# A new order for the last unit of a convolution kernel: products 1, 3, 2, 4, 5, 7, 6, 0, the turn of the unit before it between its two parts, and three steps on other engines

## The chip, the cores and the metric

The kernel runs on one core of a Trainium2 chip. Five engines work side by side, each in its own written order: TensorE (PE, matmuls and transposes; its weight loads are shown as PEld), VectorE (DVE), ScalarE (ACT), GpSimd (POOL) and SyncE (SP), which here only issues DMAs. They wait for one another through semaphores. The metric is the device time of one execution in microseconds (us).

## The reference

x has the shape (2, 2048, 1024), w has (3, 1024, 1024); all is in bfloat16. The kernel computes a convolution over the sequence with three taps, then a batch norm with given mean and variance, then silu:

```python
xp = jnp.pad(x, ((0, 0), (P, P), (0, 0)))
y = sum(jnp.einsum('bsc,cd->bsd', xp[:, k:k + S, :], w[k]) for k in range(K))
inv_std = 1.0 / jnp.sqrt(var + 1e-5)
y = (y - mean) * (g * inv_std) + b
return _silu(y)
```

## The kernel before

The convolution is done in a fast form that makes 6 outputs from 8 inputs with 8 products in place of 18. The sequence is cut into 342 tiles of 6 positions (`M_OUT`); the last tile has only 2 positions inside the sequence. At the start the inputs of each batch are transformed: for each of the 8 points j a matmul against a small matrix gives `T_sb[bi][:, ct, j, tile]`, 8 channel chunks `ct` of 128. The weights are combined per chunk of 128 output channels into six combined sets (`wts`, tile `uch`); points 0 and 7 use the raw taps (`wch`).

A *unit* is one chunk of output channels (`dc`, 8 of them) for one batch (`bi`, 2): 16 units. A unit does eight products; product j is 8 matmuls (L250), one for each `ct`, which add up in one PSUM bank. PSUM is one tile, `ps_all`, of 8 banks of 512 columns. A unit uses four banks, A, B, C and G, and units alternate between banks 0 to 3 and 4 to 7. Products 1 and 2 go to A, 3 and 4 to B, 5 and 6 to C, 7 to G and 0 to A. Each of the three pairs gives a sum and a difference: the second product is added onto the first in the bank, and the first alone (`m1`, `m3`, `m5`) is copied out before that by ScalarE. From `m1` and A come `s1`, the sum, and `d1`, twice `m1` less the sum; for the other two pairs VectorE writes twice m less the bank back into the bank. VectorE then adds the pieces, with factors, into six outputs y[0] to y[5] (`scalar_tensor_tensor`, written `stt`). ScalarE applies the norm and silu in one ACTIVATE (`silu`, L261), into `yT` in bfloat16, with channels on the partitions. The outputs lie in `y` in the order 2, 4, 1, 3, 5, 0 (`ENDS`) in the last two units, so that `silu(..., 0, 2)` does outputs 2 and 4 and `silu(..., 2, 6)` the other four.

The result must be turned so that positions are on partitions. Units 1 to 14 are turned by a DMA transpose. The fifteenth unit and the last, sixteenth, are turned by TensorE (`turn_tiles`, L465): transposes of 128 by 128 into bfloat16 views of PSUM banks (`turn_view`; 768 bfloat16 elements are 384 columns of a bank), which are then copied to SBUF and stored by DMAs on SP's queue.

The kernel is written with a manual schedule: on every engine the instructions stand in the order in which the program issues them. Waits between engines follow from the tiles that are read and written, in program order.

The change lies in the last unit (L453 to L570). It is cut into two parts along the tiles: columns 0 to 228 (`cut` is 229) and columns 229 to 341 (113 of them). Both parts are written by the generator `last_part` (L478), which yields after every matmul; `run(gen, n)` takes n matmuls of it, with what stands between them. `hooks` names places where ScalarE gets a silu that was left over: the fifteenth unit's two silus (`late`), or those of the parts themselves. The last unit's first part uses banks 4 to 7 (`here`), its second part banks 0 to 3 (`there`), the banks in which the fifteenth unit was summed.

In the order of the program, before:

- First part, products 1, 3, 5, 2, 4, 6 and half of 7 (`run(first, 52)`). The fifteenth unit's silus stand ahead of `m1`'s copy and behind `s1`'s copy (L507). `d1` is made by VectorE (L506). VectorE's work on y follows from L510.
- The stores of unit 13 (five DMAs on SP's queue).
- The turn of the fifteenth unit: 18 transposes into the upper columns (128 to 511) of banks 0, 1 and 3 and three copies into `o_before` (named `o_sb` in the profile; L544), the first two by ScalarE, the third by VectorE.
- The rest of the first part: half of product 7, product 0.
- The fifteenth unit's stores (five DMAs on SP's queue, L410 and L414).
- Second part: the same eight products on 113 columns in banks 0 to 3, with the first part's silus ahead of `m3` and behind `s1`, and its own first silu after the even outputs.
- The turn of the last unit: three blocks of tiles, 0 to 127, 128 to 228 (both from the first part) and 229 to 341. Block 0 is copied by ScalarE, block 1 by VectorE (L562), and each is stored right behind its copy; the last block is copied by VectorE in three pieces (L566, L568, L569), outputs 2 and 4 first, and then stored.

`store_block` (L467) issues a block's rows on SP's queue in a multiple of 16; five rows that are left of block 1 and the two positions of the last tile go out from ScalarE's queue (L473, L476).

Of the kernel before, what the change touches and what calls it, by code (L numbers as in the profile page):

```python
# [9 lines left out]
ALU = mybir.AluOpType  # L10
# [17 lines left out]
ALPHA = -1.0 / 20.0  # L28
# [9 lines left out]
def kernel(  # L38
# [10 lines left out]
    nc = tc.nc  # L49
# [6 lines left out]
    NTB = (S + M_OUT - 1) // M_OUT  # L56
# [3 lines left out]
    NB = (NTB + P - 1) // P  # L60
# [182 lines left out]
    def mms(bk, j, dc, bi, c0, c1, start):  # L243

        for ct in range(CT):
            if j in (0, 7):
                lhsT = raw[dc][0 if j == 0 else 2][:, ct, :]
            else:
                lhsT = wts[dc][:, j - 1, ct, :]
            nc.tensor.matmul(  # L250
                ps_all[:, bk * 512:bk * 512 + c1 - c0],
                lhsT=lhsT,
                rhs=T_sb[bi][:, ct, j, c0:c1],
                start=start and ct == 0,
                stop=ct == CT - 1,
                skip_group_check=not start,
            )
            yield

    def silu(dc, yT, y_all, c0, c1, i0, i1, step=1):  # L260
        nc.scalar.activation(  # L261
            yT[:, i0:i1:step, c0:c1],
            y_all[:, i0:i1:step],
            ACT.Silu,
            bias=beta[:, dc:dc + 1],
            scale=sk[:, dc:dc + 1],
        )
# [71 lines left out]
    def run(gen, n=None):  # L339
        while n is None or n > 0:  # L340
            if next(gen, run) is run:
                return
            if n is not None:
                n -= 1

    units = [(dc, bi) for dc in range(DC) for bi in range(B)]
    late = []
    with tc.tile_pool(name="xwin", bufs=10) as xpool:
# [19 lines left out]
        first = unit(0, 0, 0, NTB, (0, 1, 2, 3), yTs[0], late, seven_first=True)  # L368
# [21 lines left out]
    def rows(bi, n0, n1):  # L390
        r0 = bi * S
        return out_f[r0 + n0 * M_OUT:r0 + n1 * M_OUT]
# [9 lines left out]
    def store_unit(dc, bi, block):  # L402

        dcols = slice(dc * P, (dc + 1) * P)
        for nb in range(NB):
            n0, n1 = nb * P, min((nb + 1) * P, FULL)
            cuts = [n0, n1] if (n1 - n0) % 16 == 0 else [n0, n1 - (n1 - n0) % 16, n1]
            for a, z in zip(cuts, cuts[1:]):
                dst = rows(bi, a, z)[:, dcols].rearrange("(n i) d -> n i d", i=M_OUT)
                nc.sync.dma_start(out=dst, in_=block(nb)[a - n0:z - n0])  # L410
        if S % M_OUT:
            n0 = (NB - 1) * P
            dst = out_f[bi * S + FULL * M_OUT:(bi + 1) * S, dcols].rearrange("(n i) d -> n i d", i=S % M_OUT)
            nc.sync.dma_start(out=dst, in_=block(NB - 1)[FULL - n0:FULL - n0 + 1, 0:S % M_OUT])  # L414
# [10 lines left out]
    for ui, (dc, bi) in enumerate(units[1:-1], 1):  # L425
        yT = yTs[ui % 2]
# [25 lines left out]
    dc, bi = units[-1]  # L452
    yT = yTs[(len(units) - 1) % 2]  # L453
    half = 4 * ((len(units) - 1) % 2)
    here, there = [half + k for k in range(4)], [4 - half + k for k in range(4)]
    dcols = slice(dc * P, (dc + 1) * P)

    def turn_view(bk, at=0):
        pv = ps_all[:, bk * 512 + at:bk * 512 + at + M_OUT * P // 2]
        return pv.bitcast(BF16).rearrange("p (i d) -> p i d", d=P)  # L460

    def turn_tiles(pv, yT, n0, n1, k0=0, k1=M_OUT):

        for k in range(k0, k1):
            nc.tensor.transpose(pv[0:n1 - n0, ENDS[k]], yT[:, k, n0:n1], ident)  # L465

    def store_block(n0, n1, o_end):  # L467
        n2 = min(n1, FULL)
        n3 = n2 - (n2 - n0) % 16
        for a, z, queue in ((n0, n3, nc.sync), (n3, n2, nc.scalar)):  # L470
            if z > a:
                dst = rows(bi, a, z)[:, dcols].rearrange("(n i) d -> n i d", i=M_OUT)
                queue.dma_start(out=dst, in_=o_end[a - n0:z - n0])  # L473
        if n1 > FULL:
            dst = out_f[bi * S + FULL * M_OUT:(bi + 1) * S, dcols].rearrange("(n i) d -> n i d", i=S % M_OUT)
            nc.scalar.dma_start(out=dst, in_=o_end[FULL - n0:FULL - n0 + 1, 0:S % M_OUT])  # L476

    def last_part(c0, c1, banks, y_all, hooks):  # L478

        nn = c1 - c0  # L480
        A, B_, C_, G = [ps_all[:, k * 512:k * 512 + nn] for k in banks]
        bA, bB, bC, bG = banks
        m1, m3, m5, s1, d1 = (epool.tile([P, NTB], FP32, name=n)[:, 0:nn] for n in ("m1", "m3", "m5", "s1", "d1"))
        y = [y_all[:, ENDS.index(i)] for i in range(M_OUT)]

        def stt(o, i0, f, i1, op1=ALU.add):
            nc.vector.scalar_tensor_tensor(out=o, in0=i0, scalar=f, in1=i1, op0=ALU.mult, op1=op1)  # L487

        def at(name):
            for f in hooks.get(name, ()):  # L490
                f()

        def mm(bk, j, start):
            return mms(bk, j, dc, bi, c0, c1, start)

        at("m1")
        yield from mm(bA, 1, True)
        nc.scalar.copy(m1, A)
        at("m3")
        yield from mm(bB, 3, True)  # L500
        nc.scalar.copy(m3, B_)  # L501
        at("m5")
        yield from mm(bC, 5, True)
        nc.scalar.copy(m5, C_)
        yield from mm(bA, 2, False)
        stt(d1, m1, 2.0, A, op1=ALU.subtract)  # L506
        nc.scalar.copy(s1, A)  # L507
        at("s1")
        yield from mm(bB, 4, False)
        for i, f in ((2, 4.0), (4, 16.0), (0, 1.0)):  # L510
            stt(y[i], B_, ALPHA * f, s1)
        stt(B_, m3, 2.0, B_, op1=ALU.subtract)
        yield from mm(bC, 6, False)
        for i, f in ((2, 0.25), (4, 0.0625), (0, 1.0)):
            stt(y[i], C_, BETA * f, y[i])
        at("y24")
        stt(C_, m5, 2.0, C_, op1=ALU.subtract)
        for i in (5, 1, 3):
            stt(y[i], B_, ALPHA * 2.0 ** i, d1)
        for i in (5, 1, 3):  # L520
            stt(y[i], C_, BETA * 0.5 ** i, y[i])
        yield from mm(bG, 7, True)
        nc.vector.tensor_tensor(y[5], G, y[5], op=ALU.add)
        yield from mm(bA, 0, True)
        nc.vector.tensor_tensor(y[0], A, y[0], op=ALU.add)
        at("y")


    cut = FULL - 7 * 16
    y1 = endpool.tile([P, M_OUT, cut], FP32, name="y_end0")  # L530
    blocks = [(n, min(n + P, cut)) for n in range(0, cut, P)]
    ends = [endpool.tile([P, M_OUT, P], BF16, name=f"o_end{k}") for k in range(len(blocks) + 1)]
    o_before = opool.tile([P, M_OUT, NB, P], BF16, name="o_sb")

    first = last_part(0, cut, here, y1, {"m1": late[0:1], "s1": late[1:2]})
    run(first, 52)
    while turned:
        store_unit(*turned.pop(0))
    for nb, bk in enumerate((there[0], there[1], there[3])):
        n0, n1 = nb * P, min((nb + 1) * P, NTB)  # L540
        pv = turn_view(bk, 512 - M_OUT * P // 2)
        turn_tiles(pv, yTs[len(units) % 2], n0, n1)
        copy = nc.vector.tensor_copy if nb == NB - 1 else nc.scalar.copy
        copy(o_before[0:n1 - n0, :, nb], pv[0:n1 - n0])  # L544
    run(first)
    store_unit(*units[-2], lambda nb: o_before[:, :, nb])

    y2 = epool.tile([P, M_OUT, NTB], FP32, name="y")[:, :, 0:NTB - cut]
    second = last_part(cut, NTB, there, y2, {
        "m3": [lambda: silu(dc, yT, y1, 0, cut, 0, 2)],  # L550
        "s1": [lambda: silu(dc, yT, y1, 0, cut, 2, 6)],
        "y24": [lambda: silu(dc, yT, y2, cut, NTB, 0, 2)],
    })
    run(second)
    for k, (n0, n1) in enumerate(blocks):
        turn_tiles(turn_view(here[k]), yT, n0, n1)
    nn = NTB - cut
    pv, rest = turn_view(here[2]), turn_view(here[3])
    turn_tiles(pv, yT, cut, NTB, 0, 2)
    for k, copy in enumerate((nc.scalar.copy, nc.vector.tensor_copy)):  # L560
        n0, n1 = blocks[k]
        copy(ends[k][0:n1 - n0], turn_view(here[k])[0:n1 - n0])  # L562
        store_block(n0, n1, ends[k])
        if k == 0:
            silu(dc, yT, y2, cut, NTB, 2, 6)
    nc.vector.tensor_copy(ends[2][0:nn, 2:5:2], pv[0:nn, 2:5:2])  # L566
    turn_tiles(rest, yT, cut, NTB, 2, 6)
    nc.vector.tensor_copy(ends[2][0:nn, 1:6:2], rest[0:nn, 1:6:2])  # L568
    nc.vector.tensor_copy(ends[2][0:nn, 0], rest[0:nn, 0])  # L569
    store_block(cut, NTB, ends[2])  # L570


# [28 lines left out]
```

## Time and profile before

| | us |
|---|---|
| median of 3 runs | 192.84 (192.5 to 193.61) |
| the profiled execution | 193.53 |
| its span, first to last instruction | 191.7 |
| TensorE busy | 180.0 |
| VectorE busy | 161.3 |
| first matmul of the last unit's first part, second part | 172.78, 180.55 |
| the last addition into y ends | 186.06 |
| last block's store issued | 187.89 |
| last bytes moved | about 190.2 |

Times on the page are microseconds from the span's start. In a line of the timeline stand the start, the length, the engine, the line of the kernel, the operation, what it writes and reads (partitions x elements) and how often it was merged; in brackets the idle time ahead of it on its engine, and what ended that. The chain is followed back from the last instruction to whatever released it. A line of the waits has who waited, for whom, the total, how many times and the longest. DMA-issuing instructions (SPq, ACTq) show the time of the issue, not of the transfer; when bytes move is seen in the DMA share of short stretches.

### The profile page before, as it was taken

To read this page: it belongs to the slowest core of one execution; us is meant where nothing else is said; L and a number is where in the kernel's file an instruction comes from. 1 tells how busy PE (TensorE), PEld (TensorE's weight loads), DVE (VectorE), ACT (ScalarE), POOL (GpSimd) and SP (SyncE) were. 2 spreads that over 40 slices of the span, in tenths; PEclk is the share of its full clock that TensorE was granted. 3 is DMA by queue.
4 is the path that set the end of the run, shared out by engine and by line. 5 is a ranking of instruction groups with operands and counts; after the bars stand their busy time and mean duration, and the time that the engine had idled before them with its cause. 6 is when DMAs were issued, how large, how long until landed. Compare 5 with 4: busy or idle time off the path is not lost.

```text
span 191.7 us, 3904 instructions
## 1 busy us (share of the span) xinstructions
PE 180.0 (94%) x1404; PEld 128.0 (67%) x1404; DVE 161.3 (84%) x347; ACT 122.6 (64%) x201; POOL 148.0 (77%) x89
## 2 busy tenths in 40 slices
PE   7579999999999999999999999999999999999960
PEld 3369688866666666666666666666666666669950
DVE  6557999987999699969996999699969987788981
ACT  3747878888287726873786287638755873635770
POOL 6359999999949996999699969996999699900000
PEclk9966999999999999999999999999999999999996
DMA  4999997990608387999292989783746465566425
GB/s 124 323 369 305 329 292 202 285 221 0 123 0 170 69 184 196 275 142 202 46 192 57 205 228 243 147 180 68 168 81 151 95 143 108 124 120 160 118 66 105
DMA packets 86759, 31.72 MB, mean 165 GB/s; under 512 B 73364, under 2 KB 82580, under 8 KB 86740
## 3 DMA queue, kind: packets, MB, share of 16 engines
q1 hardware_dynamic: 86637, 31.46, 70.1%
q8 instruction: 11, 0.18, 0.4%
q14 instruction: 8, 0.07, 0.1%
q10 hardware_dynamic: 103, 0.02, 0.0%
HBM read 14.82 MB, written 8.39 MB: 121 GB/s over the span
## 4 chain that ended last, share of the span: by engine, by line
PE 84%; DVE 6%; DMA 5%; ACT 2%; SPq 1%; issue 1%; DVEq 0%; ACTq 0%
PE ps_all L250 75%; PE ps_all L225 8%; DMA xw<-in_x_dram 5%; DVE T_sb L241 3%; ACT yT L261 1%; DVE y L487 1%; PE ps_all L465 1%; SPq L215 1%; DVE y L291 0%; SPq L90 0%; DVE d L487 0%; DVE ps_all L487 0%; DVE o_end L568 0%; ACT s L507 0%; ACT m L501 0%
## 5 line engine op out<-in xcount | busy, mean ns | idle before, releaser
L250 PE MATMUL ps_all<-T_sb,uch 128*128 128x342 bf16 (+2 forms) x816 | 123.0, 299 | 0.0
L250 PEld LDWEIGHTS <-uch 128*128 128x128 bf16 x816 | 77.0, 97 | 33.2 <-issue 0.2
L261 ACT ACTIVATE yT<-y,beta,sk 128x684 bf16<-128x684 f32 (+5 forms) x46 | 44.2, 960 | 30.3 <-DVE y L291 29.6
L250 PE MATMUL ps_all<-T_sb,wch 128*128 128x342 bf16 (+2 forms) x272 | 44.0, 300 | 0.2 <-DVE T_sb L241 0.2
L291 DVE SCALAR_TENSOR_TENSOR y<-ps_all,y 128x342 f32<-128x342 f32 x90 | 41.9, 507 | 1.7 <-PE ps_all L250 0.7
L173 POOL TENSOR_TENSOR uch<-e,wch 128x1024 bf16<-128x1024 f32 x16 | 33.8, 2134 | 10.8 <-PE ps_all L250 5.9
L173 POOL TENSOR_TENSOR uch<-e,w1x 128x1024 bf16<-128x1024 f32 x16 | 33.8, 2135 | 0.6
L225 PE MATMUL ps_all<-Rm,xw 128*128 128x168 bf16 (+1 forms) x272 | 31.2, 251 | 3.2 <-DMA xw<-in_x_dram 2.8
L173 POOL TENSOR_TENSOR uch<-eh,w1x 128x1024 bf16<-128x1024 f32 x16 | 33.8, 2132 | 0.6
L250 PEld LDWEIGHTS <-wch 128*128 128x128 bf16 x272 | 25.6, 97 | 11.5 <-DVE T_sb L241 0.4
L239 ACT CAST T_sb<-ps_all 128x672 bf16<-128x672 f32 (+5 forms) x45 | 26.3, 606 | 9.4 <-PE ps_all L225 8.3
L298 ACT COPY m<-ps_all 128x342 f32<-128x342 f32 x45 | 19.9, 442 | 19.0 <-PE ps_all L250 18.3
L241 DVE CAST T_sb<-ps_all 128x672 bf16<-128x672 f32 (+3 forms) x40 | 26.3, 698 | 5.6 <-PE ps_all L225 5.2
L225 PEld LDWEIGHTS <-xw 128*128 128x128 bf16 (+1 forms) x272 | 24.6, 106 | 8.5 <-DMA xw<-in_x_dram 3.5
L291 DVE SCALAR_TENSOR_TENSOR y<-ps_all,d 128x342 f32<-128x342 f32 x45 | 20.3, 507 | 0.5
L163 POOL TENSOR_TENSOR e<-wch,w2x 128x1024 f32<-128x1024 bf16 x8 | 17.0, 2130 | 0.2
L163 POOL TENSOR_TENSOR eh<-w0x,wch 128x1024 f32<-128x1024 bf16 x8 | 17.1, 2132 | 0.1
L291 DVE SCALAR_TENSOR_TENSOR y<-ps_all,s 128x342 f32<-128x342 f32 x30 | 14.0, 508 | 3.2 <-ACT s L298 3.2
L291 DVE SCALAR_TENSOR_TENSOR d<-m,ps_all 128x342 f32<-128x342 f32 x15 | 7.6, 507 | 9.3 <-ACT s L298 9.3
L291 DVE SCALAR_TENSOR_TENSOR ps_all<-m,ps_all 128x342 f32<-128x342 f32 x30 | 15.3, 509 | 0.0
L169 DVE TENSOR_REDUCE e<-wch 128x1024 f32<-128x2048 bf16 x6 | 13.7, 2277 | 0.0
L298 ACT COPY s<-ps_all 128x342 f32<-128x342 f32 x30 | 13.1, 438 | 0.0
(65 smaller groups left out, 83.4 us busy)
## 6 DMA issues: line engine op xcount, KB each, us to landing
xw<-in_x_dram SPq DMA_DIRECT2D x30, 256.0 KB
out_dram<-o_sb SPq DMA_DIRECT2D x30, 192.0 KB
wch<-in_w_dram SPq DMA_DIRECT2D x9, 512.0 KB
out_dram<-o_sb SPq DMA_DIRECT2D x15, 120.0 KB
wch<-in_w_dram SPq DMA_DIRECT2D x6, 256.0 KB
xw<-in_x_dram SPq DMA_DIRECT2D x2, 224.0 KB
out_dram<-o_sb SPq DMA_DIRECT2D x15, 7.5 KB
out_dram<-o_sb SPq DMA_DIRECT2D x15, 0.5 KB
```

Of the source, the lines that this page charges most:

```text
L163: engine.tensor_tensor(e, a, c, op=ALU.add)
L169: nc.vector.tensor_reduce(e, taps.rearrange("p k ct d -> p ct d k"), axis=mybir.AxisListType.X, op=ALU.add)
L173: nc.gpsimd.tensor_tensor(wts[dc][:, 2 * n + (op == ALU.subtract)], outer[dc, n], odd, op=op)
L215: nc.sync.dma_start(out=xw[0:kk, :], in_=x[bi, t_lo:t_hi + 1, :])
L225: nc.tensor.matmul(banks[:, at:at + NJ * ntile], lhsT=xw[0:kk, (ct0 + c) * P:(ct0 + c + 1) * P], rhs=Rm[0:kk, :, 0:ntile], start=True, sto ...
L239: nc.scalar.copy(dst, src)
L241: nc.vector.tensor_copy(dst, src)
L250: nc.tensor.matmul(ps_all[:, bk * 512:bk * 512 + c1 - c0], lhsT=lhsT, rhs=T_sb[bi][:, ct, j, c0:c1], start=start and ct == 0, stop=ct == C ...
L261: nc.scalar.activation(yT[:, i0:i1:step, c0:c1], y_all[:, i0:i1:step], ACT.Silu, bias=beta[:, dc:dc + 1], scale=sk[:, dc:dc + 1],)
L291: nc.vector.scalar_tensor_tensor(out=o, in0=i0, scalar=s, in1=i1, op0=ALU.mult, op1=op1)
L298: nc.scalar.copy(dst, src)
L465: nc.tensor.transpose(pv[0:n1 - n0, ENDS[k]], yT[:, k, n0:n1], ident)
```

## The change

- The products of both parts come in the order 1, 3, 2, 4, 5, 7, 6, 0.
- ScalarE copies A out as `m1` with a factor of 2, and `d1` is `m1` less `s1`, made by GpSimd from SBUF; VectorE made it from A before.
- The fifteenth unit's silus move behind `s1`'s and behind `m5`'s copy. The first part runs through without a break. The fifteenth unit's turn stands between the parts, behind all of the first part's work, and VectorE makes all three copies. The first part's first silu stands ahead of this turn, its second behind the second part's `m5` copy.
- At the end VectorE copies blocks 0 and 1; the last block's outputs 1, 3 and 5 go into one bank and are copied by VectorE, outputs 2, 4 and 0 into another and are copied by ScalarE. All three blocks are stored after these copies in the program.
- The five left-over rows of block 1 are stored from GpSimd's queue; the last tile's two positions stay on ScalarE's.

```diff
-        for a, z, queue in ((n0, n3, nc.sync), (n3, n2, nc.scalar)):
+        for a, z, queue in ((n0, n3, nc.sync), (n3, n2, nc.gpsimd)):
...
-        at("m1")
         yield from mm(bA, 1, True)
-        nc.scalar.copy(m1, A)
-        at("m3")
+        nc.scalar.mul(m1, A, 2.0)
+        at("m1")
         yield from mm(bB, 3, True)
         nc.scalar.copy(m3, B_)
-        at("m5")
-        yield from mm(bC, 5, True)
-        nc.scalar.copy(m5, C_)
+        at("m3")
         yield from mm(bA, 2, False)
-        stt(d1, m1, 2.0, A, op1=ALU.subtract)
         nc.scalar.copy(s1, A)
+        nc.gpsimd.tensor_tensor(d1, m1, s1, op=ALU.subtract)
         at("s1")
         yield from mm(bB, 4, False)
...
         stt(B_, m3, 2.0, B_, op1=ALU.subtract)
+        yield from mm(bC, 5, True)
+        nc.scalar.copy(m5, C_)
+        at("m5")
+        for i in (5, 1, 3):
+            stt(y[i], B_, ALPHA * 2.0 ** i, d1)
+        yield from mm(bG, 7, True)
+        nc.vector.tensor_tensor(y[5], G, y[5], op=ALU.add)
         yield from mm(bC, 6, False)
         for i, f in ((2, 0.25), (4, 0.0625), (0, 1.0)):
             stt(y[i], C_, BETA * f, y[i])
-        at("y24")
+        at("even")
         stt(C_, m5, 2.0, C_, op1=ALU.subtract)
         for i in (5, 1, 3):
-            stt(y[i], B_, ALPHA * 2.0 ** i, d1)
-        for i in (5, 1, 3):
             stt(y[i], C_, BETA * 0.5 ** i, y[i])
-        yield from mm(bG, 7, True)
-        nc.vector.tensor_tensor(y[5], G, y[5], op=ALU.add)
         yield from mm(bA, 0, True)
         nc.vector.tensor_tensor(y[0], A, y[0], op=ALU.add)
...
-    first = last_part(0, cut, here, y1, {"m1": late[0:1], "s1": late[1:2]})
-    run(first, 52)
+    first = last_part(0, cut, here, y1, {"s1": late[0:1], "m5": late[1:2]})
+    run(first)
     while turned:
         store_unit(*turned.pop(0))
+
+    silu(dc, yT, y1, 0, cut, 0, 2)
     for nb, bk in enumerate((there[0], there[1], there[3])):
...
-        copy = nc.vector.tensor_copy if nb == NB - 1 else nc.scalar.copy
-        copy(o_before[0:n1 - n0, :, nb], pv[0:n1 - n0])
-    run(first)
+        nc.vector.tensor_copy(o_before[0:n1 - n0, :, nb], pv[0:n1 - n0])
     store_unit(*units[-2], lambda nb: o_before[:, :, nb])
...
-        "m3": [lambda: silu(dc, yT, y1, 0, cut, 0, 2)],
-        "s1": [lambda: silu(dc, yT, y1, 0, cut, 2, 6)],
-        "y24": [lambda: silu(dc, yT, y2, cut, NTB, 0, 2)],
+        "m5": [lambda: silu(dc, yT, y1, 0, cut, 2, 6)],
+        "even": [lambda: silu(dc, yT, y2, cut, NTB, 0, 2)],
     })
     run(second)
     for k, (n0, n1) in enumerate(blocks):
         turn_tiles(turn_view(here[k]), yT, n0, n1)
+        nc.vector.tensor_copy(ends[k][0:n1 - n0], turn_view(here[k])[0:n1 - n0])
+
     nn = NTB - cut
-    pv, rest = turn_view(here[2]), turn_view(here[3])
-    turn_tiles(pv, yT, cut, NTB, 0, 2)
-    for k, copy in enumerate((nc.scalar.copy, nc.vector.tensor_copy)):
-        n0, n1 = blocks[k]
-        copy(ends[k][0:n1 - n0], turn_view(here[k])[0:n1 - n0])
+    even, odd = turn_view(here[2]), turn_view(here[3])
+    turn_tiles(even, yT, cut, NTB, 0, 2)
+    silu(dc, yT, y2, cut, NTB, 2, 6)
+    turn_tiles(odd, yT, cut, NTB, 2, 5)
+    turn_tiles(even, yT, cut, NTB, 5, 6)
+    nc.vector.tensor_copy(ends[2][0:nn, 1:6:2], odd[0:nn, 1:6:2])
+    nc.scalar.copy(ends[2][0:nn, 0:5:2], even[0:nn, 0:5:2])
+    for k, (n0, n1) in enumerate(blocks):
         store_block(n0, n1, ends[k])
-        if k == 0:
-            silu(dc, yT, y2, cut, NTB, 2, 6)
-    nc.vector.tensor_copy(ends[2][0:nn, 2:5:2], pv[0:nn, 2:5:2])
-    turn_tiles(rest, yT, cut, NTB, 2, 6)
-    nc.vector.tensor_copy(ends[2][0:nn, 1:6:2], rest[0:nn, 1:6:2])
-    nc.vector.tensor_copy(ends[2][0:nn, 0], rest[0:nn, 0])
     store_block(cut, NTB, ends[2])
```

More of the change, by code (lines that the diff above doesn't have):

```diff
@@ L494, in mm @@
             return mms(bk, j, dc, bi, c0, c1, start)
+        yield from mm(bA, 1, True)
+        nc.scalar.mul(m1, A, 2.0)
         at("m1")
-        yield from mm(bA, 1, True)
-        nc.scalar.copy(m1, A)
-        at("m3")
         yield from mm(bB, 3, True)
         nc.scalar.copy(m3, B_)
-        at("m5")
-        yield from mm(bC, 5, True)
-        nc.scalar.copy(m5, C_)
+        at("m3")
         yield from mm(bA, 2, False)
-        stt(d1, m1, 2.0, A, op1=ALU.subtract)
         nc.scalar.copy(s1, A)
+        nc.gpsimd.tensor_tensor(d1, m1, s1, op=ALU.subtract)
         at("s1")
@@ L515, in last_part @@
             stt(y[i], C_, BETA * f, y[i])
-        at("y24")
+        at("even")
         stt(C_, m5, 2.0, C_, op1=ALU.subtract)
         for i in (5, 1, 3):
-            stt(y[i], B_, ALPHA * 2.0 ** i, d1)
-        for i in (5, 1, 3):
             stt(y[i], C_, BETA * 0.5 ** i, y[i])
-        yield from mm(bG, 7, True)
-        nc.vector.tensor_tensor(y[5], G, y[5], op=ALU.add)
         yield from mm(bA, 0, True)
         nc.vector.tensor_tensor(y[0], A, y[0], op=ALU.add)
-        at("y")
     cut = FULL - 7 * 16
```

## The prediction

> **What bounds the kernel now.** First the page: engines and chain.
>
> ```profile
> PE 180.0 (94%) x1404; PEld 128.0 (67%) x1404; DVE 161.3 (84%) x347; ACT 122.6 (64%) x201; POOL 148.0 (77%) x89
> PE 84%; DVE 6%; DMA 5%; ACT 2%; SPq 1%; issue 1%; DVEq 0%; ACTq 0%
> ```
>
> TensorE carries 84% of the chain, but the change lies in the last 19 us, so the chain is read there, in order of time (start, length, what):
>
> ```profile
> 45.09 131.03 PE ps_all L250 x912
> ...
> 176.89 1.54 ACT yT L261
> ...
> 178.47 1.07 PE ps_all L465 x16
> 179.54 2.42 PE ps_all L250 x36
> ...
> 186.09 0.78 ACT yT L261
> ...
> 186.91 0.45 PE ps_all L465 x4
> ...
> 187.38 0.36 DVE o_end L568
> ```
>
> From 176.1 the chain leaves the matmuls. Who works when is in the timeline:
>
> ```profile
> 177.02 1.00 DVE L487 SCALAR_TENSOR_TENSOR y_end<-ps_all,s 128x229 f32<-128x229 f32 x3 [0.42 <-ACT s L507]
> ...
> 178.90 1.50 ACT L544 COPY o_sb<-ps_all 128x768 bf16<-128x768 bf16 x2 [0.49 <-PE ps_all L465]
> ...
> 181.27 0.54 DVE L544 COPY o_sb<-ps_all 86x768 bf16<-86x768 bf16 x1
> ...
> 183.05 0.64 DVE L487 SCALAR_TENSOR_TENSOR y<-ps_all,s 128x113 f32<-128x113 f32 x3 [0.32 <-ACT s L507]
> ```
>
> VectorE runs without a gap from 177.02 to 182.7 and from 183.05 to 186.06, when the last block of y is done (I call that moment Y). The second part's matmuls began at 180.55, long before VectorE came to them. ScalarE did two of the three copies of the fifteenth unit's turned blocks, so their banks were free by 180.40.
>
> Two waits show what orders work in one PSUM bank:
>
> ```profile
> ACT s L507 <- DVE d L487: 1.3, 2, 0.9
> PE ps_all L189 <- ACT T_sb L239: 0.6, 1, 0.6
> ```
>
> In the first, ScalarE's copy of A waits for VectorE's d1, though both only read A. In the second, the transpose of the parameters (columns 496 to 511 of bank 0) waits 0.65 us for an eviction that reads lower columns of bank 0. So two engines are kept apart by bank, not by column. The rest hangs on this.
>
> Last, the stores (stretches: length, busy of the five engines, clock, DMA share, GB/s):
>
> ```profile
> 172.00:174.00 2.00, 2.00 (x20) 1.70 (x19) 1.97 (x5) 0.82 (x1) 0.00 (x0) 1.00 0.97 210
> 186.78:187.73 0.95, 0.43 (x4) 0.29 (x4) 0.35 (x2) 0.07 (x1) 0.00 (x0) 1.00 0.97 204
> 189.05:190.20 1.15, 0.00 (x0) 0.00 (x0) 0.00 (x0) 0.00 (x0) 0.00 (x0) 0.50 0.75 149
> ```
>
> Block 0 was issued at 185.56 and its bytes moved from 186.78, 1.2 us later; the last block was issued at 187.89 and moved until 190.2.
>
> **The change, part by part.** All times are in the profiled execution, 193.53 us with a span of 191.70; that is 0.69 above the median of 192.84.
>
> *Order of products, first part.* Its matmuls start at 172.78 and follow each other by 4.73/48 = 0.0985 us, a product in 0.79. VectorE's first operation now needs product 4 as fourth, 172.78 + 32 x 0.0985 = 175.93, plus the 0.27 us that lie between a product's end and VectorE (176.21 before, after the fourth product too). So VectorE starts the y work at 176.20 instead of 177.02: d1 (0.41) and the wait for s1 (0.42) are gone from it. Product 2 needs m1 copied first: copied at 173.83 to 174.16, product 2 due at 174.36; product 4 needs m3 (174.97), due at 175.14. Cover 0.15 to 0.2, no stall. m1 becomes a scaled copy: as an ACTIVATE it costs between the copy (0.33) and a silu of that width (0.40 + 229 x 0.00083 = 0.59). I take 0.04 above the copy, from the 1024-wide scaling at L151 (1.05, at 0.83 ns an element); at the upper end about 0.1 is lost.
>
> *d1 on GpSimd.* GpSimd has no work after 167.4. By its 1024-wide operations (2.13) and the smallest (0.10), 229 columns take about 0.55 and 113 about 0.32. s1 ends at 175.75, d1 at 176.4; VectorE needs it at 177.4. In the second part the cover is 0.6. Cost nothing; d1 has nothing queued behind it.
>
> *First part on VectorE.* The 16 operations that stay took 5.40 - 0.47 (the copy among them) = 4.93, so they run from 176.20 to 181.13. Products 7, 6 and 0 end at 177.51, 178.30 and 179.09, each at least 0.07 ahead of need.
>
> *The fifteenth unit's turn.* Its silu of two slots moves behind s1 (175.66 to 176.62), that of four slots behind m5 (177.24 to 178.77). TensorE ends product 0 at 179.09 and turns at once, without the 0.29 stall of before: 18 transposes until 180.15. But all three copies are now VectorE's, in order behind the y work, at 0.46 pitch and 0.55 length (101x768 and 86x768 took 0.55): the first ends at 181.63, the second at 182.09, the third at 182.55. On VectorE that is 3 x 0.46 against the one 0.47 of before, 0.91 more. The five stores on SP's queue follow from 181.7, 0.58 to 0.74 each, and end by 185.2; SP is next needed at 187.3. Unit 13's stores stay ahead of them, issued from 175.1 as before.
>
> *The wait this adds.* The second part's products 1, 3 and 7 write the banks that these copies read. By the bank rule product 1 can't start before 181.63 + 0.05 = 181.68, where it started at 180.55: 1.13 late, and behind it in TensorE's order stand all 64 matmuls and the end's 18 transposes. A product of 113 columns takes 8 x 0.0538 = 0.43, an end reaches ScalarE 0.24 later. Product 1 to 182.11; m1 to 182.64; product 2, held by m1, from 182.69 to 183.12; product 4 to 183.55; VectorE at 183.82, against 183.05. So VectorE, free at 182.46, stands idle for 1.36. The 16 operations took 3.01 and still do: **Y is 186.83 instead of 186.06, +0.77**. Products 5, 7, 6 and 0 stay ahead of VectorE by 0.1 or more (6 ends at 184.95, needed at 185.32). ScalarE's silu of the first part's four slots (1.16) fits between m5 and 185.6.
>
> *The end.* Before: silu 0.77, four transposes 0.43, two copies on VectorE, last end at Y + 1.80. Now VectorE first copies blocks 0 and 1 (to Y + 0.46 and Y + 0.92, under the silu and the transposes, which last to Y + 1.28; without that cover they would add up to 1.0). Then ScalarE copies 384 columns while VectorE copies the other 384. ScalarE's price lies between 0.44 (342 columns) and 0.78 (768); by their slope 0.48, which I take. Last end Y + 1.79: nothing won, nothing lost, +0.3 at the upper bound.
>
> *Store order.* Block 0 used to leave half a microsecond before Y; now all three leave after it: at Y + 0.49, Y + 1.09, Y + 1.82. First bytes at 186.83 + 0.49 + 1.2 = 188.52; the 524 KB together need 2.50 us at the 207 GB/s of two dense stretches: 191.0, against 190.2. If instead the last block found the engines free, it would end by its own issue, +0.76; at the rates of the three blocks as shown one by one (0.95, 0.95, 1.1) it would be 191.5, +1.3. The first row is a dense queue like this one, so I take it: **+0.85** in all, Y's 0.77 in it.
>
> *The five-row store on GpSimd.* It waits for the copy of block 1, 187.75; nothing stands behind it. ScalarE loses an issue of 0.93 that lay beside its silu: no gain. The trace has no DMA from GpSimd. Bounds: nothing, or a preparation as long as its 2.13 us operation, then 1.2 to first bytes and up to 1.0 in a full queue: 192.1, which would add 1.1. The small operation with the longest time there, 1.66 on 8 elements, would give 190.6 at least and is nearest in size; it is under cover until 191.0, so I take nothing.
>
> Sum: 193.53 + 0.85 = 194.38 in the profiled execution's terms, **193.7** against the median of 192.84. Its own range is 193.35 (VectorE and queue at their lower ends) to 194.3.
>
> **Where a rule is weighed.** From 7.96 to 11.37 TensorE was busy 1.55 of 3.41 us, its longest gap 1.84, and the clock fell to 0.50 at 11.37; from 4.54 to 7.96 it was busy 2.69 and the clock stayed. Here a stretch around the new wait (180.15 to 181.68) would be busy 1.88 of 3.41, 55%, between the two. The Trainium skill, page "TensorE: Matmul & The Clock Gate", section "What's actually happening", puts the drop after an idle window of about 3.4 us; by that rule the 1.5 us wait costs no clock. By the row at 11.37 a gap half as long sufficed, so the trace does not agree and the drop stays a rival.
>
> **The rivals.**
> (a) Not slower: the copies don't hold TensorE, because columns and not banks are kept apart. Then product 4 ends at 182.07, VectorE goes on at 182.46, Y = 185.47; three blocks from 187.16, 2.5 us, 189.7 against 190.2: -0.5, 192.35. It decides if product 1 can start before 180.9. For it: the copied columns (128 to 511) and the written ones (0 to 112) are disjoint; against it: the wait of L189. 0.10.
> (b) The GpSimd store lands last: from 3.3 us after 187.75 on. At the upper bound above, 194.8. For it: no row shows how fast it is; against it: 30 pieces only. 0.10. The Trainium skill, page "GPSIMD Engine Reference", section "2.1 Instruction dispatch", says that a first call to freshly loaded code pays about 6 us; if that met this store, an estimate by that page is some 3 us beyond 194.8. No run here shows it.
> (c) The clock halves over the second part: 32 matmuls before product 4's end at 0.054 more each, up to +1.7, 194.6 to 195.4. 0.06.
>
> **How the numbers follow.** Forecast 0.70, rivals 0.26, else 0.04 (0.03 of it faster). Half a per cent is 0.96 us, about what a measurement of this kernel tells from no change, and the forecast's range lies across it: 0.34 of its 0.70 above, 0.36 within. Slower 0.34 + 0.10 + 0.06 + 0.01 = 0.51; within 0.36 + 0.08 of (a) = 0.44; faster 0.05. The range goes from (a), 192.3, to (b)'s bound, 194.8; beyond lie (c)'s upper half, the slow tail of (b) and the faster cases, under 0.2.
>
> **What would show it.** TensorE idle about 1.5 us ahead of the second part's product 1, released by VectorE's copy of `o_sb`; the first y operation at 176.2; a VectorE gap of about 1.4 us ahead of the second part; last copy on ScalarE; DMA busy without a dip from 188.5 to 191. Wrong if product 1 starts ahead of the copies, if a clock of 0.50 stands before the end, or if the last bytes are GpSimd's.

## The result and the profile after

The changed kernel is slower: 194.60 us against 192.71 us in the medians, a ratio of 1.0106 with a 95% interval of 1.0071 to 1.0141. The forecast was 193.7, from a median of 192.84 in the three runs known then, so the direction was right and the size a little under half of what came.

The two profiled executions can't be compared by the clock of the page alone, because the stages ahead of the change took different times: the first matmul of the last unit's first part (I call it S) starts at 172.78 in the profile of before and at 171.74 in that of after. From S to the end of the span it is 191.70 - 172.78 = 18.92 us before and 192.60 - 171.74 = 20.86 after: 1.94 more, which agrees with the medians (1.89). Below, all times of a kernel are given from its own S.

The chain of the changed kernel in the stretch in question (start, length, what):

```profile
175.15 1.00 DVE y_end L491 x3
...
180.43 0.47 DVE o_sb L548
...
180.94 1.55 PE ps_all L250 x24
```

It goes over VectorE's work on y, then through VectorE's first copy of the fifteenth unit (line 548), and only from there to the matmuls of the second part. (Its last pieces are on GpSimd: `d1` of the second part, 4.20 us without work, then its store. That store isn't what the end waits for, see below.) The timeline shows both waits of this step, and the places where VectorE lost more time than the forecast gave it:

```profile
175.15 1.00 DVE L491 SCALAR_TENSOR_TENSOR y_end<-ps_all,s 128x229 f32<-128x229 f32 x3 [0.28 <-PE ps_all L250]
176.07 0.39 DVE L491 SCALAR_TENSOR_TENSOR ps_all<-m,ps_all 128x229 f32<-128x229 f32 x1
176.56 1.00 DVE L491 SCALAR_TENSOR_TENSOR y_end<-ps_all,d 128x229 f32<-128x229 f32 x3
...
178.69 0.39 DVE L491 SCALAR_TENSOR_TENSOR ps_all<-m,ps_all 128x229 f32<-128x229 f32 x1
179.12 1.00 DVE L491 SCALAR_TENSOR_TENSOR y_end<-ps_all,y_end 128x229 f32<-128x229 f32 x3
...
180.34 1.47 DVE L548 COPY o_sb<-ps_all 128x768 bf16<-128x768 bf16 x3
180.94 2.39 PE L250 MATMUL ps_all<-T_sb,uch 128*128 128x113 bf16 x40 [1.73 <-DVE o_sb L548]
...
183.03 0.64 DVE L491 SCALAR_TENSOR_TENSOR y<-ps_all,s 128x113 f32<-128x113 f32 x3 [1.22 <-PE ps_all L250]
183.59 0.27 DVE L491 SCALAR_TENSOR_TENSOR ps_all<-m,ps_all 128x113 f32<-128x113 f32 x1
183.97 0.64 DVE L491 SCALAR_TENSOR_TENSOR y<-ps_all,d 128x113 f32<-128x113 f32 x3
...
186.11 0.27 DVE L529 TENSOR_TENSOR y<-ps_all,y 128x113 f32<-128x113 f32 x1
```

VectorE starts on y at 175.15, S + 3.41, where the kernel before started at S + 4.24: this gain came. TensorE then stands idle for 1.73 until VectorE's first copy is done, and VectorE stands idle for 1.22 until product 4 of the second part. Y, the end of the last addition, is 186.38: S + 14.64, against S + 13.28 before.

In the second, third, fourth and fifth of these lines a write into a bank is followed by operations that read that bank. The first pair starts 0.49 apart and the second 0.43, where two independent operations of this width start 0.30 apart. The second part has two such pairs as well (183.59 and 183.97 here, and later 185.25 and 185.55): 0.38 and 0.30 apart, where independent operations start 0.18 to 0.19 apart.

The stores (stretch: length, busy of the five engines, clock, DMA share, GB/s) and GpSimd's own (size and time from issue to landing):

```profile
188.10:190.90 2.80, 0.00 (x0) 0.00 (x0) 0.00 (x0) 0.07 (x1) 0.27 (x1) 0.74 0.93 186
```

```profile
out_dram<-o_end POOLq DMA_DIRECT2D x1, 7.5 KB, 3.1
```

The three blocks leave as one queue, as forecast, but at 186 GB/s and not 207. GpSimd's store was issued at 187.61, so it landed at 190.7, inside the time of the last block's bytes. The clock of 0.74 in the first of these lines is a mean: it falls to 0.50 at about 189.4, behind the last matmul, which ends at 187.7.

### The profile page after: what moved, and what is told of

Its sections match the earlier page's. It is cut to its first block, busy times and chain, and to the rows that moved or that the text cites. A ratio compares the mean times of both kernels' runs of the same rounds, so it can differ in the third digit from the quotient of the medians.

```text
span 192.6 us, 3902 instructions
## 1 busy us (share of the span) xinstructions
PE 178.2 (93%) x1404; PEld 125.5 (65%) x1404; DVE 162.2 (84%) x346; ACT 120.8 (63%) x199; POOL 149.8 (78%) x92
## 4 chain that ended last, share of the span: by engine, by line
PE 79%; DMA 10%; DVE 4%; issue 3%; POOLq 0%; POOL 0%; SPq 0%; ACT 0%; DVEq 0%; ACTq 0%
PE ps_all L250 74%; DMA xw<-in_x_dram 10%; PE ps_all L225 5%; DVE y_end L491 2%; DVE T_sb L241 1%; DVE y L291 0%; POOLq L597 0%; DVE ps_all L491 0%; DVE o_sb L548 0%; POOL d L508 0%; SPq L90 0%; DVE y_end L529 0%; DVE y_end L520 0%; ACT s L507 0%; DVE ps_all L291 0%
## 5 line engine op out<-in xcount | busy, mean ns | idle before, releaser
L225 PE MATMUL ps_all<-Rm,xw 128*128 128x168 bf16 (+1 forms) x272 | 29.3, 236 | 4.6 <-DMA xw<-in_x_dram 4.3
L225 PEld LDWEIGHTS <-xw 128*128 128x128 bf16 (+1 forms) x272 | 22.0, 99 | 10.4 <-DMA xw<-in_x_dram 5.8
L508 POOL TENSOR_TENSOR d<-m,s 128x229 f32<-128x229 f32 (+1 forms) x2 | 1.1, 554 | 15.9 <-ACT s L507 15.9
```

Of the source, the lines that this page charges most:

```text
L225: nc.tensor.matmul(banks[:, at:at + NJ * ntile], lhsT=xw[0:kk, (ct0 + c) * P:(ct0 + c + 1) * P], rhs=Rm[0:kk, :, 0:ntile], start=True, sto ...
L508: nc.gpsimd.tensor_tensor(d1, m1, s1, op=ALU.subtract)
```

## The experiments

Eight kernels ran, five changed from the kernel after (e), one from the kernel before (b), and two that combine edits (f). "Y" and "end" are from each kernel's own S; the end is that of the span. S lay between 171.2 and 173.6 in these profiles; nothing ahead of it was edited, so its scatter is left out in this way. The ratio is to the kernel before, run on the same chip.

| kernel | S | Y | end | ratio (95%) |
|---|---|---|---|---|
| before | 172.78 | 13.28 | 18.9 | 1 |
| changed | 171.74 | 14.64 | 20.9 | 1.0106 (1.0071 to 1.0141) |
| b1: before, VectorE makes the three copies | 171.64 | 14.64 | 20.4 | 1.0077 (1.0046 to 1.0108) |
| e1: other banks for the turn | 171.22 | 13.32 | 19.5 | 1.0028 (0.9999 to 1.0057) |
| e5: ScalarE makes two copies | 171.53 | 13.96 | 20.5 | 1.0049 (1.0018 to 1.0081) |
| e2: one operation between write and reader | 173.55 | 14.00 | 20.1 | 1.0066 (1.0028 to 1.0105) |
| e3: block 0 copied by ScalarE | 171.53 | 14.64 | 20.4 | 1.0087 (1.0056 to 1.0118) |
| e4: five rows from ScalarE's queue | 172.33 | 14.64 | 21.1 | 1.0119 (1.0079 to 1.0159) |
| f1: e1, e2 and e3 together | 171.40 | 12.71 | 18.4 | 0.9975 (0.9955 to 0.9996) |
| f5: f1, one copy by ScalarE | 171.80 | 12.42 | 18.7 | 0.9992 (0.9969 to 1.0016) |

Y and end come from one profile of each kernel. By the times alone, the intervals of e2, e3, e4 and e5 overlap with that of the changed kernel, so what is said of these four rests on the rows of their profiles; e1 and f1 are clear of the changed kernel, and b1 is clear of the kernel before.

The theory was that VectorE's copies hold TensorE, because two engines are kept apart in one PSUM bank. The rivals were that VectorE's added work alone counts, or that it is VectorE's order whoever owns the bank. For the part of the loss that the forecast had missed, the theory was a late start of an operation that reads what the one ahead of it wrote, and a longer queue of stores.

### e1: the turn in banks that the second part needs late or never

```diff
-    for nb, bk in enumerate((there[0], there[1], there[3])):
+    for nb, bk in enumerate((there[2], there[3], here[3])):
```

> The changed kernel (1.0106 of the kernel before), but the fifteenth unit is turned into banks 2, 3 and 7 in place of 0, 1 and 3. The copies stay VectorE's, at the same place. Theory (the copies hold TensorE by bank): product 1 of the second part starts right behind the transposes, at 7.2 us after the first part's first matmul in place of 9.10; the idle of 1.73 on TensorE and of 1.22 on VectorE is gone; VectorE goes on right behind its third copy, so the time falls by 1.1 to 1.2 us, to about 1.0045. Rival (what costs is the work that was moved onto VectorE, and the hold lies beside it): the time stays at 1.0106 within 0.2 us. Rival (columns are kept apart, and product 1 waited for something else that ended with the copy): the wait of TensorE stays.

TensorE and VectorE of this kernel, timeline:

```profile
177.53 1.17 PE L465 MATMUL ps_all<-ident,yT 128*128 128x128 bf16 x18
178.53 2.46 PE L250 MATMUL ps_all<-T_sb,uch 128*128 128x113 bf16 x40
```

```profile
179.82 1.47 DVE L548 COPY o_sb<-ps_all 128x768 bf16<-128x768 bf16 x3
181.21 0.63 DVE L491 SCALAR_TENSOR_TENSOR y<-ps_all,s 128x113 f32<-128x113 f32 x3
```

The matmuls follow the transposes with no idle bracket (S + 7.31), and VectorE goes from its third copy straight into the second part. The three copies are as long as before and on the same engine. The end falls by 1.4 us (20.9 to 19.5), a little more than expected. So these 1.4 us are the price of the bank. The rival that VectorE's added work as such makes up this loss falls: that work is all still there. (It isn't free: f5 takes one of the three copies off VectorE, and Y comes 0.29 earlier.) The rival that product 1 waited for something else that ended with the copy falls too: product 1 now starts at S + 7.31, ahead of the first copy (179.82, S + 8.60). What the profile shows is a wait, so the runs tell what it costs and that it goes by bank; whether the chip itself needs it, no run here tells.

### b1: the copies alone, in the kernel before

```diff
-        copy = nc.vector.tensor_copy if nb == NB - 1 else nc.scalar.copy
-        copy(o_before[0:n1 - n0, :, nb], pv[0:n1 - n0])
+        nc.vector.tensor_copy(o_before[0:n1 - n0, :, nb], pv[0:n1 - n0])
```

> The kernel before, with one part of the change alone: VectorE makes all three copies of the fifteenth unit's turned blocks, at their old place and in their old banks (0, 1, 3). Theory (the copies in VectorE's order hold TensorE by bank): product 1 of the second part starts behind VectorE's first copy, about 9.1 us after the first part's first matmul in place of 7.77; product 2, now held too, is the fourth, product 4 the fifth; VectorE comes to the second part's y about 1.2 us later than at 10.27; the time rises by 1.1 to 1.3 us, to about 1.0062. Rival (only VectorE's added work of 0.93 counts, and much of it fills the second part's waits): 0.4 to 0.6 us, 1.0025.

TensorE and VectorE of b1, then VectorE's last operation of the first part in the kernel before:

```profile
180.74 2.74 PE L250 MATMUL ps_all<-T_sb,uch 128*128 128x113 bf16 x48 [1.16 <-DVE o_sb L543]
```

```profile
181.83 0.38 DVE L525 TENSOR_TENSOR y_end<-ps_all,y_end 128x229 f32<-128x229 f32 x1
182.69 0.28 DVE L487 SCALAR_TENSOR_TENSOR d<-m,ps_all 128x113 f32<-128x113 f32 x1 [0.47 <-ACT m L504]
```

```profile
182.04 0.38 DVE L525 TENSOR_TENSOR y_end<-ps_all,y_end 128x229 f32<-128x229 f32 x1
```

This one edit of the old kernel brings 1.4 of the change's 1.9 us, a little more than expected, and the same kind of wait, product 1 at S + 9.10. The new order of the products isn't needed for the loss. But the 1.4 us are not the wait alone: VectorE ends the first part at S + 10.57 in place of 9.64, 0.93 later by the copies that were added to it, and only then stands idle for 0.47, because TensorE was held. So in this kernel the added work counts in full and the wait adds about half a microsecond to it.

### e5: ScalarE's copies again, at the new place

```diff
-        nc.vector.tensor_copy(o_before[0:n1 - n0, :, nb], pv[0:n1 - n0])
+        copy = nc.vector.tensor_copy if nb == NB - 1 else nc.scalar.copy
+        copy(o_before[0:n1 - n0, :, nb], pv[0:n1 - n0])
```

> The changed kernel, with ScalarE making the first two copies again, at the new place between the parts and in the old banks. Theory (it is the bank, whoever copies): ScalarE is busy with the first part's first silu until 7.5 us after the first part's first matmul, its copies end at 8.3 and 9.1, so product 3 is held until 9.1 by bank 1 and m1 stands behind the copies in ScalarE's order; the second part's y starts at about 10.8 in place of 11.3, and the time falls by 0.5 only, to about 1.008. Rival (it is VectorE's order alone): the whole 1.3 is won, 1.0035, as with other banks.

```profile
178.98 1.48 ACT L549 COPY o_sb<-ps_all 128x768 bf16<-128x768 bf16 x2
179.81 2.64 PE L250 MATMUL ps_all<-T_sb,uch 128*128 128x113 bf16 x40 [0.80 <-ACT o_sb L549]
...
180.47 0.27 ACT L501 ACTIVATE m<-ps_all 128x113 f32<-128x113 f32 x1
...
182.15 0.64 DVE L491 SCALAR_TENSOR_TENSOR y<-ps_all,s 128x113 f32<-128x113 f32 x3 [1.47 <-PE ps_all L250]
```

Now it is ScalarE's copy that TensorE waits for, and m1 stands behind both copies. Y falls by 0.7 and not by the 1.3 of e1; the end falls by 0.4. The ratio doesn't decide here: 1.0049 lies between the 1.008 of the theory and the 1.0035 of the rival, and its interval holds both. By the rows it isn't VectorE in particular: whoever copies out of the bank holds it, and the new place, between the parts, is late for either engine.

### e2: one operation between a write and its first reader

```diff
-        for i, f in ((2, 4.0), (4, 16.0), (0, 1.0)):
+        for i, f in ((2, 4.0), (4, 16.0)):
             stt(y[i], B_, ALPHA * f, s1)
-        stt(B_, m3, 2.0, B_, op1=ALU.subtract)
+        stt(m3, m3, 2.0, B_, op1=ALU.subtract)
+        stt(y[0], B_, ALPHA, s1)
...
-            stt(y[i], B_, ALPHA * 2.0 ** i, d1)
+            stt(y[i], m3, ALPHA * 2.0 ** i, d1)
```

(The same for C_ and m5.)

> The changed kernel, but the differences of the second and third pair are written into m3 and m5 in SBUF, one operation earlier, so that one operation (the third even output) stands between the write and its first reader on VectorE. Same count of operations. Theory (an operation that reads what the operation right ahead of it wrote starts 0.11 to 0.19 us late; four such places make up 0.6 of the miss): the first part's 16 operations take 4.95 in place of 5.28, the second's 3.05 in place of 3.35, and the time falls by 0.5 to 0.6, to about 1.0077. Rival (the gap behind the write of B is the wait for GpSimd's difference): the two gaps at B stay, only those at C go, and the time falls by 0.25.

```profile
177.58 0.39 DVE L491 SCALAR_TENSOR_TENSOR m<-m,ps_all 128x229 f32<-128x229 f32 x1
177.88 0.39 DVE L491 SCALAR_TENSOR_TENSOR y_end<-ps_all,s 128x229 f32<-128x229 f32 x1
178.18 1.00 DVE L491 SCALAR_TENSOR_TENSOR y_end<-m,d 128x229 f32<-128x229 f32 x3
```

The operations are as many and as long as before, and those of 229 columns now start 0.30 apart, also the one that needs GpSimd's difference. The first part's sixteen take 181.93 - 176.96 = 4.97 in place of 5.28, the second's 187.55 - 184.50 = 3.05 in place of 3.35; Y and the end fall by 0.6 and 0.7. The rival that VectorE waited for GpSimd at B falls: the gap there went without GpSimd's result coming any earlier (it was done at S + 3.73 in both kernels, about 1 us ahead of its reader). In this kernel the difference of the pair also moved from PSUM to SBUF, so the run doesn't tell by itself that distance and not place did it. The profile of the kernel before fills this gap in two ways. In its last unit the same write into bank B stands ahead of an operation that doesn't read it. And its fifteenth unit has dependent pairs of both kinds: 173.06 and 173.60 through a bank, 174.88 and 175.41 through y[0] in SBUF.

```profile
177.94 0.39 DVE L487 SCALAR_TENSOR_TENSOR ps_all<-m,ps_all 128x229 f32<-128x229 f32 x1
178.24 0.99 DVE L487 SCALAR_TENSOR_TENSOR y_end<-ps_all,y_end 128x229 f32<-128x229 f32 x3
```

```profile
173.06 0.51 DVE L291 SCALAR_TENSOR_TENSOR ps_all<-m,ps_all 128x342 f32<-128x342 f32 x1
173.60 1.36 DVE L291 SCALAR_TENSOR_TENSOR y<-ps_all,y 128x342 f32<-128x342 f32 x3
```

```profile
174.45 0.50 DVE L291 SCALAR_TENSOR_TENSOR y<-ps_all,y 128x342 f32<-128x342 f32 x1
174.88 0.50 DVE L291 SCALAR_TENSOR_TENSOR y<-s,ps_all 128x342 f32<-128x342 f32 x1
175.41 0.51 DVE L291 SCALAR_TENSOR_TENSOR y<-ps_all,y 128x342 f32<-128x342 f32 x1
```

With no reader behind it, the write into the bank is followed after 0.30, where the changed kernel shows 0.49 and 0.43. Of the 342-column operations an independent pair (174.45, 174.88) is 0.43 apart, the dependent pair through SBUF 0.53 and the one through the bank 0.54. So it is the distance and not the place.

### e3: block 0 of the end stored early

```diff
-        "even": [lambda: silu(dc, yT, y2, cut, NTB, 0, 2)],
...
-        nc.vector.tensor_copy(ends[k][0:n1 - n0], turn_view(here[k])[0:n1 - n0])
+        copy = nc.vector.tensor_copy if k else nc.scalar.copy
+        copy(ends[k][0:n1 - n0], turn_view(here[k])[0:n1 - n0])
+    silu(dc, yT, y2, cut, NTB, 0, 2)
```

> The changed kernel, but ScalarE copies block 0, ahead of the silu of outputs 2 and 4 of the second part; VectorE copies block 1 alone. Theory (the three stores queue on the DMA engines from Y + 1.7 on, and that costs 0.4 beyond Y): block 0 is issued about 1.0 earlier, the last block's bytes end 0.4 earlier against Y, and the time falls by 0.4, to about 1.0085. Rival (the end is set by the last block's own issue): the time stays.

Y is unchanged at S + 14.64, and the first of the three stores is issued at 185.83, S + 14.30, in place of S + 15.13. The end falls by 0.5. The DMA engines now stand still from about 189.0 to 189.2, so the last block finds them free and its bytes follow its own issue. So the stores' queue costs about half a microsecond beyond Y.

### e4: the five rows from ScalarE's queue

```diff
-        for a, z, queue in ((n0, n3, nc.sync), (n3, n2, nc.gpsimd)):
+        for a, z, queue in ((n0, n3, nc.sync), (n3, n2, nc.scalar)):
```

> The changed kernel, but the five rows of block 1 go out from ScalarE's queue, as before. Theory (the store on GpSimd lands at 190.7, beside the last block's bytes): no change, 1.0106 within 0.2 us. Rival (it lands last, or the end waits for GpSimd): the time falls by 0.2 or more, and the time from the last bytes to the end of the span falls from 1.6 to 1.5 or less.

No gain: 1.0119 against 1.0106, with intervals that overlap almost wholly. In this arrangement ScalarE's last store is issued 1.05 behind the first one on its queue (188.35 and 189.40), which may be why the span is 0.2 longer; the times don't tell that apart. The rival's second sign didn't come either: the last bytes move until about 191.6, and from there to the end of the span it is 1.8 us and not 1.5 or less. But as the rows now leave later, from a queue with another store behind them, this run alone doesn't clear GpSimd's store; that it landed at 190.7, ahead of the last block's bytes, does.

### f1: the three edits together

> The changed kernel with the three edits that won alone: other banks for the fifteenth unit's turn, the differences written to SBUF one operation earlier, block 0 of the end copied by ScalarE. If the three are separate, their gains add up (1.38, 0.71 and 0.49 us in the stretch from the first part's first matmul to the end of the span): 18.3 us for this stretch against 18.92 in the kernel before, and a ratio of about 0.997. If they cover for each other (VectorE waits for TensorE once it starts earlier), 0.3 to 0.5 less, 0.999.

The gains add up: the end is S + 18.4, against 18.9 before, and the ratio is 0.9975 (0.9955 to 0.9996). It is the only version whose interval stays below one, and only just; the gain is a quarter of a per cent. So the change as a whole is worth something once its banks, its order on VectorE and its stores are put right. No run takes the new order of the products or the difference on GpSimd alone, so what each gives isn't shown. The rival that the edits cover for each other falls: VectorE runs without a gap from the first part's y to Y (12.71).

### f5: one of the copies on ScalarE

```diff
-    silu(dc, yT, y1, 0, cut, 0, 2)
...
-        nc.vector.tensor_copy(o_before[0:n1 - n0, :, nb], pv[0:n1 - n0])
+        copy = nc.vector.tensor_copy if nb else nc.scalar.copy
+        copy(o_before[0:n1 - n0, :, nb], pv[0:n1 - n0])
...
+        "s1": [lambda: silu(dc, yT, y1, 0, cut, 0, 2)],
```

(At the end the silu of outputs 2 and 4 stands ahead of ScalarE's copy of block 0.)

> As the kernel with three edits, and ScalarE makes the first copy of the fifteenth unit, ahead of the first part's first silu, which moves behind the second part's s1; at the end ScalarE's silu of outputs 2 and 4 stands ahead of its copy of block 0. VectorE comes to the second part 0.25 us earlier (9.46 after the first part's first matmul in place of 9.73); at the end the last silu may start 0.15 late behind the copy. Expected: 0.1 to 0.25 us below the kernel with three edits; if ScalarE's copy delays m1, nothing.

Y came 0.29 earlier, a little more than the 0.25 expected on VectorE, but the end didn't: 18.7 against 18.4. The last copies end earlier too (S + 14.3 against 14.5), so the difference lies behind the copies, in the stores. Why they took longer stays open, and by the times (0.9992, 0.9969 to 1.0016) this kernel can't be told apart from f1.

## Why the prediction was right in its direction and half in its size

Point by point, from S:

- *Order of products.* VectorE's start on y was forecast at 3.42 and came at 3.41; no stall on TensorE.
- *The wait that the change adds.* Product 1 behind VectorE's copy, by the bank: forecast at 8.90, came at 9.20, released by the copy of `o_sb`. e1 shows that it is the cause and what it costs in this kernel, 1.3 us of Y and 1.4 us of the end; b1 shows the same wait without the new order, where it adds 0.47 us to 0.93 us of work. VectorE's gap was forecast at 1.36 and came at 1.22, because its own first part ran late (next point). Rival (a), that columns and not banks are kept apart, is out.
- *"They run from 176.20 to 181.13" and "The 16 operations took 3.01 and still do".* This is the first step of the sum that failed. The same sixteen operations stand in another order, in which four of them read what the operation right ahead of them wrote. They took 5.28 in place of 4.93 and 3.35 in place of 3.01. Y was forecast at 14.05 and came at 14.64; of these 0.59 e2 wins back all. The price was on the page before, in the pair at 174.88 and 175.41 above; I took sums over groups and didn't ask what stood next to what.
- *Store order.* The second term that was too small. Issues came nearly as forecast (Y + 0.49 for the first, Y + 1.90 in place of 1.82 for the last), but the 524 KB took 2.8 us and not 2.50 (at its 207 GB/s they are 2.53, which the sum of 0.85 goes by), and the end came 6.22 after Y, where 5.64 + 0.08 = 5.72 was forecast. I had a range of 0.76 to 1.3 for the sum and took a value near its lower end; with the late operations left out, the upper end would have been about right (1.94 - 0.59 = 1.35). e3 shows that the queue as such is worth half a microsecond. The 2.8 us explain about 0.3 of the 0.50; the rest lies in the last few KB and between the last bytes and the end of the span, and no run here takes it apart.
- The two together are 0.59 + 0.50 = 1.09, the whole difference between 0.85 and 1.94: the path was right, and two terms of the sum were too small.
- *The end.* Last copy at Y + 1.80, forecast Y + 1.79: the two engines at the last block won nothing.
- *The five rows on GpSimd.* Issued in 0.76, landed after 3.1, under cover by 0.2 or so; e4, without it, was no faster. Rival (b) is out, and the 6 us that the Trainium skill's page "GPSIMD Engine Reference" names for a first call to freshly loaded code in its section "2.1 Instruction dispatch" was not met here. (The prediction's estimate with these 6 us, "some 3 us beyond 194.8", is 3.9 by the terms of its own bound, and 2.9 only without the full queue.)
- *d1 on GpSimd.* 0.68 and 0.43 in place of 0.55 and 0.32, hidden all the same: it ended at 175.47 and 183.39, and its readers start at 176.56 and 183.97.
- *The clock.* It was 1.00 through the wait and after it, so rival (c) is out; the 0.50 from about 189.4 on stands behind the last matmul, as it does in the kernel before, and costs nothing. In this place the rule of the Trainium skill's page "TensorE: Matmul & The Clock Gate", section "What's actually happening", agrees with the trace: 1.73 us of idle cost no clock.

```profile
175.15:180.43 5.28, 4.06 (x50) 3.90 (x48) 5.14 (x17) 2.96 (x4) 0.32 (x1) 1.00 0.42 99
180.43:183.03 2.60, 2.09 (x38) 2.02 (x38) 1.38 (x3) 0.77 (x3) 0.07 (x1) 1.00 0.30 72
183.03:186.38 3.35, 2.81 (x44) 2.27 (x41) 3.21 (x17) 1.88 (x3) 0.36 (x1) 1.00 0.45 106
```

The clock column of the stretches, third from the right, stays at 1.00 across TensorE's idle time (179.2 to 180.94) and in the stretch that follows.

## What to carry to other kernels

When a copy out of PSUM moves to another engine or behind other work, look up which later matmul writes the same bank, even in other columns, and price the move by when that matmul may start, not by the copy's length; another bank can be worth more than another engine (1.4 us in e1 against 0.4 in e5). When operations on one engine change their order, check each neighbouring pair for a read of what was just written and add 0.1 to 0.2 us for each, which is what it cost here at 113 to 342 columns. At the end of a kernel, stores that used to leave one by one and now leave together have to be priced as one queue.

## What was not expected of the hardware

- On VectorE independent operations overlap: the next starts 0.07 to 0.09 us ahead of the end of the one before. A dependent one starts 0.03 to 0.11 behind that end, so each such pair costs 0.10 to 0.19 (0.10 to 0.11 at 342 columns, 0.12 to 0.13 and 0.18 at 229, 0.11 and 0.19 at 113). The larger values stand where the reader also needs GpSimd's result. There the chain has a short wait on VectorE's queue (`176.50 0.02 DVEq L491`) and none ahead of the reader of C; that this second wait makes the difference was only argued. The Trainium skill, page "VectorE: DVE Perf Modes", section "The DRAIN you can't avoid", says that the next operation doesn't start until the pipe is empty, but that one which is not held starts earlier. The independent pairs here agree with the second half. The same section says that a semaphore between two operations costs nothing extra; no run here shows whether that holds for this second wait.
- The transfer rate of the three queued blocks isn't even: 200 to 250 GB/s over the first 0.7 us, about 140 to 210 over the next 1.4 us, and over 200 again in the last 0.4 us, also in e1 and e2. What slows it was not tried.
